# A list-scheduled sparse attention and feed-forward kernel: its planner gives each kind of DMA transfer its own share beside the weights, and the order is found anew

## The chip, the cores and the metric

The kernel runs on one core of a Trainium2 chip. The metric is the device time of one execution in microseconds. Five engines work from queues of their own: TensorE (PE, with its weight loads PEld), VectorE (DVE), ScalarE (ACT), GpSimd (POOL) and SyncE (SP). Each queue runs in the order in which it was written; engines wait for each other by semaphores. Transfers between HBM and SBUF are issued by SP, by ACT (four of them) and by GpSimd (the weights, which are cast to bf16 on the way).

## The reference

Attention over 4 batches of 8 heads, 768 positions and head dimension 64, where each query sees only its 6 best chunks of 32 keys; then a feed-forward layer on the 3072 tokens.

```python
ub = sum_d max(q * k_min[chunk], q * k_max[chunk])   # bound per query and chunk
ub = where(causal over chunks, ub, -1e9); top_chunks = the 6 largest
scores = q @ k.T / 8, masked to the chosen chunks and to the past
x = softmax(scores) @ v                               # tokens x 512
h = x @ w_in                                          # 512 -> 2048
out = (h * clip(h + 3, 0, 6) / 6) @ w_out             # 2048 -> 512
```

## The kernel before

The work is cut into 16 attention units (4 batches, two halves of the positions, two quads of heads; a unit is two pairs of heads) and 8 dense groups (batch and half: 384 tokens).

Attention of a unit: K and Q are loaded (`load_quad`, line 229, for batch 0; `load`, line 237, for the others in four parts each, KS and QS) and turned (line 375 on TensorE for batch 0; `KF` and `QF`, line 387, on VectorE for the others). VectorE takes minimum and maximum of each chunk of K (KMA, lines 400 to 403). TensorE forms the bounds (UBT, line 442), VectorE finds the 6 best chunks (lines 447 to 472), TensorE the scores (SPS, line 494 for batch 0, where the array is split by rows, line 497 for the others), ScalarE their exponentials (PT, line 507), GpSimd cuts the triangle of the diagonal (line 512), TensorE multiplies by V (PVP, line 530), and VectorE divides by the sums (Xb, line 542). V is loaded at lines 243 (VS, batch 0) and 248 (VT).

A dense group: its tokens are turned (XT, on TensorE at line 551, or for five groups through DRAM: BT, BD and BF, lines 561 to 580), then 16 times HP (four matmuls each, line 587), U (ScalarE, line 592) and GT (VectorE, line 595), then three times OP (16 matmuls each, line 602; the very last tile is cut in two, line 610), which is scaled and stored (lines 628 and 634). HP needs a half of WIN, OP needs a half of WOUT: the first 8 of its 16 matmuls the first half, the others the second.

Nothing of this order is written by hand. Every step is given to a `Plan` (`add`) with the engines that may run it and a length for each, a rank, the steps it waits for, and the buffers it takes and gives: four PSUM banks "m", two for scores, tiles in SBUF, and eight lanes for transfers under way. `order` then plays the steps as a list schedule: whenever an engine comes free in its own reckoning, the ready step with the lowest rank and with room goes next. The result is the order of each engine's queue; on the chip only the queue order and the semaphores are left. So every number in the plan (a rank, a length, a share) can change the order of all queues behind it. Ranks come from the unit or group, from the table RANK, and from the table SHIFT, which adds to the rank of single steps by their number.

The plan has a line of its own for transfers ("DMA") and one for weights ("WT"). While weights are under way or waiting, another transfer is reckoned at a fraction of its speed, 0.15, until the weights are through.

When a weight half is issued is ruled by a gate: GpSimd first copies one element of a tile that another transfer writes (`seen`, line 313), and only then issues the half (lines 316 and 319).

```python
GATE = dict(I0="V2", I1="I0", O0="I1", O1="O0")
```

I0 and I1 are the halves of WIN, O0 and O1 those of WOUT; V2 is the third unit's V. So before, each half is issued after the one ahead of it has landed.

Fillers: up to 45 us of the plan's time, where the plan sees TensorE idle for over 0.25 us, small matmuls on unused PSUM columns are put in (`occupy`, line 365).

Of the kernel before, what the change touches and what calls it, by code (L numbers as in the profile page):

```python
# [12 lines left out]
ACT = mybir.ActivationFunctionType  # L13
# [11 lines left out]


SHIFT = {
# [18 lines left out]
}  # L46


class Plan:
# [10 lines left out]
        self.room, self.steps = {kind: list(range(n)) for kind, n in room.items()}, []  # L60
        self.lane, self.lanes, self.lean = 0, room["lane"], {}

    def add(self, engine, length, rank, run=None, after=(), take=(), give=(), port=False, tiles=None, lock=None):


        step = dict(lengths=engine if isinstance(engine, dict) else {engine: length}, rank=(rank + SHIFT.get(len(self.steps), 0), len(self.steps)),
                    run=run, told=isinstance(engine, dict), port=port, tiles=tiles, lock=lock, take=take, give=give, then=[])
        step["wait"] = {e: len(after) for e in step["lengths"]}
        for other in after:
            other["then"].append(step)  # L70
        self.steps.append(step)
        return step
# [21 lines left out]
    def order(self, **busy):  # L94
# [19 lines left out]
        n = len(events)  # L114
        while events:
# [8 lines left out]
            for e, steps in ready.items():  # L124
                if free[e] > now + 1e-9:
                    continue
                for st in sorted(steps, key=lambda x: x["rank"][:1] if e == "DMA" else x["rank"]):
                    if "engine" in st:
                        steps.remove(st)
                    elif self.sooner(st, e, free, now):  # L130
                        continue
                    elif self.room_for(st):
                        steps.remove(st)
                        for held in st["take"]:
                            held[2] = self.take(held[0])
                        out.append(st)
                        begin = now
                        if e == "POOL" or e == "DVE" and st["port"]:
                            begin = max(now, port["DVE" if e == "POOL" else "POOL"])
                            port[e] = begin + st["lengths"][e]  # L140
                        begin = max(begin, locks.get(st["lock"], 0.0))
                        if e == "PE":
                            begin += 0.1 * (st["tiles"] != tiles)
                            tiles = st["tiles"]
                        length = st["lengths"][e]
                        if e == "PE" and begin < self.COLD:
                            length *= 1.9
                        if e == "DMA":
                            weights = max(free["WT"] - now, 0.0) + sum(x["lengths"]["WT"] for x in ready["WT"])
                            length = min(length / 0.15, weights + max(length - 0.15 * weights, 0.0))  # L150
                        st["at"], st["engine"], st["length"] = begin, e, length
                        free[e] = begin + st["length"]
                        if st["lock"]:
                            locks[st["lock"]] = free[e] + 0.12
                        n += 2
                        heapq.heappush(events, (free[e], n, st, True))
                        heapq.heappush(events, (free[e] + self.BEHIND[e], n + 1, st, False))
                        break
# [10 lines left out]
def kernel(  # L169
# [466 lines left out]


    SEQ = "K0 Q0 K1 Q1 Q3 Q2 K2 V1 V0 V2 K3 V3"
    GATE = dict(I0="V2", I1="I0", O0="I1", O1="O0")
    RANK = dict(lead2=-64.96, lead3=-10.65, rdense=58.76, step=10.99, fs=-0.34, rt=-2000.0, rw=-1999.0, lead=-10.68, sel=-8.96, opoff=45.01, opsp=1.83, tri=24.62, joint=-38.37, vals=-12.37, eb=-0.8, lp=-0.13, la=0.2, kc=5.02)  # L640
    plan = Plan(m=4, s=2, kf=3, qf=6, qr=6, ub=3, mt=3, pt=9, x=2, xt=2, bt=2, bd=2, gt=2, u=3, ot=2, vt=3, ks=2, qs=2, lane=8)
    plan.room["gt"].remove(1)
    add = plan.add
# [11 lines left out]
    def arrive(engine, issue, length, run, after=(), take=(), parts=1):  # L655
# [3 lines left out]
        for part in range(parts):  # L659
# [6 lines left out]
            if engine == "POOL":  # L666
                issued.append(got)
                got = add("GEN", 1.2, 0, after=[got])
            landed.append(add("WT" if engine == "POOL" else "DMA", length, 0, after=[got], give=lane))
        return landed  # L670

    held_inputs = {}
# [218 lines left out]
    for what in ("I0", "I1", "O0", "O1"):  # L891
        name, n = dict(I="WIN", O="WOUT")[what[0]], int(what[1])
        got, seen = landing[GATE[what]]
        there[name, n] = arrive("POOL", 0.95, 6.6 if name == "WIN" else 7.6, (load_weights, name, n, seen), after=got[-1:])
        landing[what] = there[name, n], lambda name=name, n=n: WIN[0:1, KT_HID - 1, n * DFF // 2:n * DFF // 2 + 1] if name == "WIN" else WOUT[0:1, n * FT // 2, 0:1]

    r = RANK["rdense"]
    for n_group, ((b, half), xs) in enumerate(finished.items()):
# [3 lines left out]
        if (b, half) in WORDS:  # L902
# [3 lines left out]
                                  take=[held_bt] if quad == 0 else [], give=[x]))  # L906
            lane = hold("lane")
            kept = add("SP", 0.37, -3000, later(keep_words, g), after=before, take=[held_bd, lane])
            kept, m = add("DMA", 1.4, 0, after=[kept], give=[held_bt, lane]), []
            for part in range(4):  # L910
                lane = hold("lane")
                m.append(add("SP", 0.43, -3000, later(fetch_words, g, part), after=[kept] + m[-1:], take=[held_bf, lane] if part == 0 else [lane]))
# [16 lines left out]
        for t in range(HB):  # L929
            prev = []  # L930
            m, ot = hold("m"), hold("ot")
            if b == B - 1 and half == 1 and t == HB - 1:
                m[1] = ot[1] = 2
                for part in range(2):
# [2 lines left out]
                    a = add(dict(ACT=0.36, DVE=0.35), None, r + RANK["rt"], later(result_last_out, g, t, part), after=prev, take=[] if part else [ot], give=[m])  # L937
                    lane = hold("lane")
                    a = add("SP", 0.37, -2000, later(result_last_store, g, t, part), after=[a], take=[lane])
                    add("DMA", 0.6, 0, after=[a], give=[ot, lane])  # L940
                continue
            for part in range(4):
                prev = [add("PE", 0.865, r + RANK["opoff"] + RANK["opsp"] * (4 * t + part), later(result, g, t, part),
# [2 lines left out]
            a = add(dict(ACT=0.56, DVE=0.66), None, r + RANK["rt"], later(result_scale, g, t), after=prev, take=[ot], give=[m])  # L946
            lane = hold("lane")
            a = add("SP", 0.37, -2000, later(result_out, g, t, nc.sync), after=[a], take=[lane])
            add("DMA", 0.75, 0, after=[a], give=[ot, lane])
        r += RANK["step"]  # L950
    for step in (steps := plan.order(PE=3.7, ACT=4.25, DVE=4.4, POOL=3.2, SP=3.7, DMA=1.6, WT=1.6)):
        chosen = {}
        for kind, _, number in step["take"]:
            chosen.setdefault(kind, []).append(number)
# [36 lines left out]
```

## Time and profile before

| | us |
|---|---|
| median of three runs | 272.17 (272.03 to 273.77) |
| the profiled execution | 271.37 |
| its span, first to last instruction | 269.7 |
| TensorE busy | 256.8 (95%) |
| VectorE busy | 209.4 (78%) |
| ScalarE busy | 191.6 (71%) |
| GpSimd busy | 128.7 (48%) |

The page gives busy time and share of the span of each engine, the span in 40 slices, the DMA queues, the chain of work that ended last, and the costliest groups of instructions with the idle time ahead of them. Matmuls are pipelined: a matmul's recorded time overlaps with the next one's, so what a matmul costs is better read from the time of a long run of them, divided by their count. TensorE's clock was granted in full in all 40 slices.

### The profile page before, as it was taken

The numbers are of one execution on the slowest core, as the hardware profiler recorded it, in microseconds if no ns is written. First come the engines' busy times: TensorE is split into PE (matmuls) and PEld (weight loads), VectorE is DVE, ScalarE is ACT, GpSimd is POOL, SyncE is SP. The second block draws the span as 40 slices with busy tenths as digits, with TensorE's granted clock in tenths as the row PEclk, the third lists the DMA queues.
The fourth block names the chain that finished last, engine by engine and source line by source line (L and its number), as shares of the span: only waits on it lengthen the run. The fifth ranks groups of instructions, "written<-read, shape, count | busy, mean of one in ns | idle before, by whom it ended". The sixth has DMA issues, their size and how long they took to land.

```text
span 269.7 us, 6517 instructions
## 1 busy us (share of the span) xinstructions
PE 256.8 (95%) x2350; PEld 152.7 (57%) x2373; DVE 209.4 (78%) x588; ACT 191.6 (71%) x306; POOL 128.7 (48%) x289
## 2 busy tenths in 40 slices
PE   7997999898999999999999999999999999999994
PEld 4645565654445677644664566654665756555443
DVE  7799898989799997899989999999894424857000
ACT  3589899685527899765984499953998874868021
POOL 4168579533767485559734666752842310200000
PEclk9999999999999999999999999999999999999999
DMA  8999999999948999954995599114103003201122
GB/s 166 219 198 188 190 175 154 176 149 185 212 108 117 127 157 176 186 164 139 150 159 141 157 155 181 40 60 139 39 4 117 5 38 139 58 0 41 39 78 79
DMA packets 122720, 33.71 MB, mean 125 GB/s; under 512 B 113216, under 2 KB 118080, under 8 KB 122688
## 3 DMA queue, kind: packets, MB, share of 16 engines
q1 hardware_dynamic: 117952, 28.71, 62.2%
q0 software_dynamic: 3136, 4.19, 9.5%
q10 hardware_dynamic: 1600, 0.39, 0.7%
q8 instruction: 18, 0.29, 0.6%
q14 instruction: 14, 0.11, 0.2%
HBM read 29.23 MB, written 8.26 MB: 139 GB/s over the span
## 4 chain that ended last, share of the span: by engine, by line
PE 73%; DMA 10%; DVE 8%; SPq 4%; ACT 2%; issue 1%; ACTq 0%; DVEq 0%
PE OP L602 28%; PE HP L587 23%; PE SPS L497 9%; DMA KS<-in_k_dram 8%; PE PVP L530 6%; PE UBT L442 4%; SPq L229 2%; DVE GT L595 2%; PE SPS L494 2%; DMA VS<-in_v_dram 2%; ACT PT L507 1%; PE OP L610 1%; SPq L237 1%; DVE KMA L401 1%; DVE KMA L400 1%
## 5 line engine op out<-in xcount | busy, mean ns | idle before, releaser
L587 PE MATMUL HP<-XT,WIN 128*128 128x384 bf16 x512 | 92.4, 326 | 2.4 <-DVE GT L595 2.3
L507 ACT ACTIVATE PT<-SPS 128x1024 bf16<-128x1024 f32 (+1 forms) x96 | 85.3, 927 | 12.0 <-PE SPS L497 9.9
L602 PE MATMUL OP<-WOUT,GT 128*128 128x512 bf16 x345 | 82.3, 379 | 1.9 <-issue 0.5
L592 ACT ACTIVATE U<-HP,THREE 128x384 bf16<-128x384 f32 x128 | 73.0, 594 | 15.1 <-PE HP L587 8.8
L595 DVE SCALAR_TENSOR_TENSOR GT<-U,HP 128x384 bf16<-128x384 bf16 x128 | 67.2, 545 | 14.9 <-ACT U L592 11.0
L587 PEld LDWEIGHTS <-WIN 128*128 128x128 bf16 x512 | 48.5, 98 | 34.4 <-issue 4.0
L602 PEld LDWEIGHTS <-GT 128*128 128x128 bf16 x368 | 35.1, 98 | 40.2 <-issue 3.7
L512 POOL TENSOR_SCALAR_AFFINE_SELECT PT<-PT 128x256 bf16<-128x256 bf16 x96 | 38.9, 418 | 35.9 <-ACT PT L507 34.9
L497 PE MATMUL SPS<-QLA,KL 128*128 128x384 bf16 (+2 forms) x240 | 36.3, 278 | 0.0
L628 ACT ACTIVATE OT<-OP 128x512 f32<-128x512 f32 x22 | 13.1, 597 | 27.4 <-PE OP L602 27.0
L331 POOL TENSOR_SCALAR_AFFINE_SELECT KL<-KF 64x384 bf16<-64x384 f32 x48 | 23.9, 501 | 14.4 <-DVE KF L387 12.1
L331 POOL TENSOR_SCALAR_AFFINE_SELECT QLA<-QF 64x384 bf16<-64x384 f32 x48 | 24.6, 512 | 12.2 <-DVE QF L387 6.3
L497 PEld LDWEIGHTS <-KL 128*128 128x128 bf16 x240 | 21.7, 98 | 12.8 <-issue 0.6
L530 PEld LDWEIGHTS <-PT 128*128 128x128 bf16 x672 | 23.9, 97 | 3.1 <-issue 0.4
L530 PE MATMUL PVP<-VB,PT 128*128 128x65 bf16 x672 | 25.6, 194 | 0.0
L411 ACT ACTIVATE QR<-QF 128x384 f32<-128x384 f32 x30 | 15.4, 531 | 9.4 <-DVE QF L387 9.3
L542 DVE TENSOR_TENSOR Xb<-PVP,RINV 128x384 bf16<-128x384 f32 x32 | 18.5, 579 | 1.1
L580 POOL COPY XT<-BF 128x384 bf16<-128x384 bf16 x20 | 9.3, 504 | 16.7 <-DMA BF<-BD 16.6
L536 DVE RECIPROCAL RINV<-PVP 128x6 f32<-128x6 f32 x32 | 5.9, 185 | 12.6 <-PE PVP L530 12.2
L387 DVE STREAM_TRANSPOSE KF<-KS 128x384 f32<-128x384 f32 x24 | 13.2, 560 | 1.7 <-DMA KS<-in_k_dram 1.3
L387 DVE STREAM_TRANSPOSE QF<-QS 128x384 f32<-128x384 f32 x24 | 12.8, 555 | 2.0 <-DMA QS<-in_q_dram 2.0
L400 DVE TENSOR_REDUCE KMA<-KF 128x12 f32<-128x384 f32 x24 | 13.1, 545 | 0.4
(80 smaller groups left out, 235.8 us busy)
## 6 DMA issues: line engine op xcount, KB each, us to landing
out_dram<-OT SPq DMA_DIRECT2D x23, 256.0 KB, 2.3
KS<-in_k_dram SPq DMA_DIRECT2D x24, 192.0 KB, 5.5
QS<-in_q_dram SPq DMA_DIRECT2D x24, 192.0 KB, 6.5
VT<-in_v_dram SPq DMA_DIRECT2D x24, 192.0 KB, 4.5
WIN<-in_moe_w_in_dram POOLq DMA_DIRECT2D x2, 1024.0 KB, 9.4
WOUT<-in_moe_w_out_dram POOLq DMA_DIRECT2D x2, 1024.0 KB, 10.1
BD<-BT SPq DMA_DIRECT2D x5, 384.0 KB, 2.4
BF<-BD SPq DMA_DIRECT2D x20, 96.0 KB, 2.3
```

Of the source, the lines that this page charges most:

```text
L331: nc.gpsimd.affine_select(out=to, in_=x, pattern=[[0, n]], compare_op=A.is_ge, fill=0.0, base=0, channel_multiplier=0)
L387: nc.vector.transpose(T[:], st[name][:, st["i"], half * HC:(half + 1) * HC, :].rearrange("p c e -> p (c e)"))
L400: nc.vector.tensor_reduce(out=over, in_=chunks, axis=X_AXIS, op=A.max)
L497: nc.tensor.matmul(SP[:, j, c0:c0 + n], lhsT=KLS[st["pair"] % 6][:, j, jb * P:(jb + 1) * P], rhs=st["QL", half][:, j, at:at + n], start=Tr ...
L507: nc.scalar.activation(PT[:, :, 0:cols], SP[:, :, 0:cols], ACT.Exp, scale=scale)
L512: nc.gpsimd.affine_select(out=PT[:, :, c0:c0 + P], in_=PT[:, :, c0:c0 + P], pattern=[[0, 2], [1, P]], compare_op=A.is_ge, fill=0.0, base=0 ...
L530: nc.tensor.matmul(PVP[:, j, n, :], lhsT=PT[:, j, c0:c0 + P], rhs=st["VB"][:, jb, j, :], start=(jb == 0), stop=(jb == qb))
L542: nc.vector.tensor_tensor(out=to, in0=PVP[:, :, :, 0:D], in1=RINV[:].to_broadcast([P, 2, HB, D]), op=A.mult)
L587: nc.tensor.matmul(HP[:], lhsT=WIN[:, kt, f * P:(f + 1) * P], rhs=g["XT"][:, kt, :, :], start=(kt == 0), stop=(kt == KT_HID - 1))
L592: nc.scalar.activation(U[:], g["HP", f][:], ACT.Relu, bias=THREE[:], scale=1.0)
L595: nc.vector.scalar_tensor_tensor(out=g["GT"][:, f, :], in0=g["U", f][:], scalar=6.0, in1=g["HP", f][:], op0=A.min, op1=A.mult)
L602: nc.tensor.matmul(g["OP", t][:], lhsT=g["GT"][:, f, t * P:(t + 1) * P], rhs=WOUT[:, f, :], start=(f == 0), stop=(f == FT - 1))
```

## The change

`add` takes a share for each step, and `order` uses it in place of 0.15. Input transfers with a length over 1 (the parts of K and Q of batches 1 to 3) get 0.09, the shorter ones 0.18, the store to DRAM of the turned groups 0.45, output stores 0.4, and all others 0.2. The lengths of the weights go from 6.6 and 7.6 to 6.3 and 7.3. The gates become V3, Q3, Q2 and O0: the first WIN half waits for the last V of batch 0, the second for the fourth unit's Q, the first WOUT half for the third unit's Q (both loaded before that V), and the second WOUT half for the first, as before. The SHIFT table is replaced whole (other steps, other numbers). The computation, its tiles and buffers stay. With these numbers the plan comes to another order on all five queues.

```diff
 SHIFT = {
-    4: -885.8, 6: -49.2, 8: -980.9, 10: -841.2, 12: -1020.7, 14: -50.4, 16: -1.5, 18: -911.2, 20: 8.9, 22: -4.1, 28: -823.6, 30: -2.5, 32: -915.5, 40:
...
+    16: -912.2, 40: 1266.8, 46: 1213.1, 89: 152.4, 91: 137.3, 99: 176.2, 100: -2962.9, 102: 115.3, 110: -1915.9, 120: 31.5, 123: -1888.8, 126: 110.3, 133:
...
 }
...
-    def add(self, engine, length, rank, run=None, after=(), take=(), give=(), port=False, tiles=None, lock=None):
+    def add(self, engine, length, rank, run=None, after=(), take=(), give=(), port=False, tiles=None, lock=None, share=0.2):
...
-                            length = min(length / 0.15, weights + max(length - 0.15 * weights, 0.0))
+                            length = min(length / st["share"], weights + max(length - st["share"] * weights, 0.0))
...
-    GATE = dict(I0="V2", I1="I0", O0="I1", O1="O0")
+    GATE = dict(I0="V3", I1="Q3", O0="Q2", O1="O0")
...
-            landed.append(add("WT" if engine == "POOL" else "DMA", length, 0, after=[got], give=lane))
+            landed.append(add("WT" if engine == "POOL" else "DMA", length, 0, after=[got], give=lane, share=0.09 if length > 1 else 0.18))
...
-        there[name, n] = arrive("POOL", 0.95, 6.6 if name == "WIN" else 7.6, (load_weights, name, n, seen), after=got[-1:])
+        there[name, n] = arrive("POOL", 0.95, 6.3 if name == "WIN" else 7.3, (load_weights, name, n, seen), after=got[-1:])
...
-            kept, m = add("DMA", 1.4, 0, after=[kept], give=[held_bt, lane]), []
+            kept, m = add("DMA", 1.4, 0, after=[kept], give=[held_bt, lane], share=0.45), []
...
-                    add("DMA", 0.6, 0, after=[a], give=[ot, lane])
+                    add("DMA", 0.6, 0, after=[a], give=[ot, lane], share=0.4)
...
-            add("DMA", 0.75, 0, after=[a], give=[ot, lane])
+            add("DMA", 0.75, 0, after=[a], give=[ot, lane], share=0.4)
```

More of the change, by code (lines that the diff above doesn't have):

```diff
@@ L61, in __init__ @@
         self.lane, self.lanes, self.lean = 0, room["lane"], {}
-    def add(self, engine, length, rank, run=None, after=(), take=(), give=(), port=False, tiles=None, lock=None):
+    def add(self, engine, length, rank, run=None, after=(), take=(), give=(), port=False, tiles=None, lock=None, share=0.2):
         step = dict(lengths=engine if isinstance(engine, dict) else {engine: length}, rank=(rank + SHIFT.get(len(self.steps), 0), len(self.steps)),
-                    run=run, told=isinstance(engine, dict), port=port, tiles=tiles, lock=lock, take=take, give=give, then=[])
+                    run=run, told=isinstance(engine, dict), port=port, tiles=tiles, lock=lock, share=share, take=take, give=give, then=[])
         step["wait"] = {e: len(after) for e in step["lengths"]}
@@ L948 @@
             a = add("SP", 0.37, -2000, later(result_out, g, t, nc.sync), after=[a], take=[lane])
-            add("DMA", 0.75, 0, after=[a], give=[ot, lane])
+            add("DMA", 0.75, 0, after=[a], give=[ot, lane], share=0.4)
         r += RANK["step"]
-    for step in (steps := plan.order(PE=3.7, ACT=4.25, DVE=4.4, POOL=3.2, SP=3.7, DMA=1.6, WT=1.6)):
+    steps = plan.order(PE=3.7, ACT=4.25, DVE=4.4, POOL=3.2, SP=3.7, DMA=1.6, WT=1.6)
+    for step in steps:
         chosen = {}
```

32 rows, old and new, of the table SHIFT are left out of this document.

## The prediction

> **What bounds the kernel now.** I read the page first, then windows cut at marks of the TensorE queue, then the chain, TensorE's waits and the queues by time.
>
> ```profile
> span 269.7 us, 6517 instructions
> ...
> DMA  8999999999948999954995599114103003201122
> ...
> 20.00:35.60 15.60, 13.55 (x215) 8.63 (x206) 13.92 (x53) 13.70 (x22) 10.97 (x23) 1.00 1.18 187
> 35.60:65.30 29.70, 27.18 (x270) 16.54 (x267) 26.91 (x58) 24.77 (x40) 17.70 (x39) 1.00 1.25 169
> 65.30:72.60 7.30, 7.23 (x43) 3.48 (x49) 6.66 (x14) 3.67 (x8) 3.46 (x9) 1.00 1.26 186
> 72.60:266.10 193.50, 191.83 (x1687) 113.37 (x1708) 145.97 (x409) 136.71 (x216) 88.67 (x193) 1.00 0.57 105
> ```
>
> A window's columns are its length, then busy time of PE, PEld, DVE, ACT and POOL. From 72.6 to 266.1 us TensorE idles 1.67 us of 193.5, at full clock (1.00). Both kernels hold the same matmuls but for fillers, so there an order can win little over a microsecond. What it can win lies before 72.6 us, where the DMA engines are nearly always busy and TensorE idles 2.05 us (20 to 35.6) and 2.52 us (35.6 to 65.3).
>
> ```profile
> 32.11 1.38 PE PVP L530 x42
> ...
> 33.92 0.78 PE XTP L551 x12
> 34.70 0.98 PE SPS L494 x16
> 35.68 1.41 PE HP L587 x8
> ...
> 65.31 0.38 PE OP L602
> ...
> 68.07 1.30 PE HP L587 x8
> 69.37 1.73 PE OP L602 x8
> ```
>
> These rows of the chain (start, length, what, count) give pitches: PVP 0.033 us, XTP 0.065, a row-split score 0.061, HP 0.163 (1.30/8), OP 0.216. HP starts at 35.6, OP at 65.3. Between them the queue of before holds 116 HP (18.9 us), 90 PVP (3.0), 48 row-split scores (2.9) and 12 XTP (0.8): 25.6 us of work in 29.7. So 4.1 us are lost, partly idle, partly in matmuls stretched where the row split switches. What stands behind it:
>
> ```profile
> PE HP L587 <- DVE GT L595: 2.3, 4, 1.2
> ...
> 58.24 0.58 DVE L387 STREAM_TRANSPOSE KF<-KS 128x384 f32<-128x384 f32 x1 [0.61 <-DMA KS<-in_k_dram]
> ...
> 69.66 0.58 DVE L387 STREAM_TRANSPOSE QF<-QS 128x384 f32<-128x384 f32 x1 [0.55 <-DMA QS<-in_q_dram]
> ```
>
> HP waits for a PSUM bank; the GT that frees it stands on VectorE's queue behind KF and QF, and these wait for loads that share the DMA engines with the weights.
>
> **The change part by part.** No instruction's work changes; the order does. I counted instructions in the new queues.
>
> *The first HP comes later.* Ahead of it stand 28 more row-split scores (1.7 us), 30 more PVP (1.0) and 7 more fillers:
>
> ```profile
> 7.27 1.06 PE L365 MATMUL QT<-IDENTB 128*128 128x128 bf16 x16
> ```
>
> Sixteen fillers take 1.06 us, so seven 0.5, together 3.2 us. ScalarE has four more exponentials (and two copies fewer) ahead of its first U and VectorE seven more instructions ahead of the first XT, so no engine is much sooner there: HP at 35.6 + 3.0 = 38.6. Only the fillers are loss; the rest is work done earlier.
>
> *The weights queue up.* The gate of the first WIN half moves from V2 to V3, those of the second half and of the first WOUT half to Q3 and Q2, which land long before. So GpSimd issues the second half right behind the first, and the first WOUT half after seven more triangles, near 31 us.
>
> ```profile
> 24.89 1.00 POOL L316 DMA_DIRECT2D WIN<-in_moe_w_in_dram  x1
> ...
> 26.27 0.56 POOL L257 TENSOR_SCALAR_AFFINE_SELECT VB<-VS 128x384 bf16<-128x384 f32 x1
> ...
> 34.53 0.77 POOL L316 DMA_DIRECT2D WIN<-in_moe_w_in_dram  x1
> DMA to landing us min/median/max: 9.1/9.4/9.6
> DMA to landing us min/median/max: 9.9/10.1/10.2
> q0 software_dynamic: 3136, 4.19, 9.5%
> ```
>
> The two landings are those of WIN and WOUT. A cast that needs V3 runs at 26.27, so V3 has landed by then; in the new SP queue the last V is the 34th load too. First WIN half: issue 26.4, landed 35.8, inside the 38.6 that HP waits for anyway. A queued half is not seen in this trace. Its packets take 6.4 us (9.5% of 269.7, a quarter of it); alone it needs 9.4 to 10.1. So it follows its predecessor by 6.4 to 10.0; I take 7.3 and 7.8, nearer to the packets, because issue (0.77 to 1.00) and landing then overlap. Second WIN half 43.1, first WOUT half 50.9; the second WOUT half, still gated by the first, 51 + 10.1 = 61.1 (58.7 to 65.4).
>
> The Trainium skill, "DMA: Bandwidth & Descriptors", section "Anatomy of one DMA — SWDGE (gpsimd) path", gives a DMA from GpSimd a fixed part of about 2.0 us, mostly the write receipt. By that a queued WIN half would follow after 7.4 us, and the sum would stay as it is.
>
> *The path to the first OP.* Between first HP and first OP the new queue has 96 HP (15.6), 60 PVP (2.0), 20 row-split scores (1.2) and 12 XTP (0.8): 19.6 us. Of the 4.1 us lost before I keep 1.0, since fewer scores are mixed in and no KF or QF stands between the last twelve GT. OP starts at 38.6 + 19.6 + 1.0 = 59.2. Its ninth matmul, at 60.9, needs the second WOUT half: landed 61.1, a wait of 0.2 (0 to 4.5). What is queued behind it is all of TensorE.
>
> *The loads of batch 1.*
>
> ```profile
> 27.98 13.23 SPq L237 DMA_DIRECT2D QS<-in_q_dram  x4
> 41.31 11.22 SPq L237 DMA_DIRECT2D KS<-in_k_dram  x4
> 52.57 13.23 SPq L237 DMA_DIRECT2D QS<-in_q_dram  x4
> ...
> 86.78 7.64 SPq L237 DMA_DIRECT2D QS<-in_q_dram  x4
> ```
>
> A K or Q part takes 1.9 us of the SP queue without weights (86.78) and 2.8 to 3.3 beside them; with the gaps between the weights taken out, about 4.0. Weights without gaps until 51 cost SP some 5 us of gap, 1.5 parts. But the second K now stands at places 7 to 10 of 16 instead of 9 to 12: issued by 51, on chip near 57, and VectorE asks for it only after the GT run, near 59. The last Q parts (13 to 16) arrive near 70, as before. Meanwhile TensorE has 32 OP (6.9) and 8 HP (5.2) that need no KF. I charge 0.8 us for GT behind a late QF; without that cover it would be up to 4.
>
> *Sum.* From first OP to first UBT of batch 1 the new queue has 40 OP (8.6) and 32 HP (5.2): 13.8 us, so UBT at 59.2 + 0.2 + 13.8 + 0.8 = 74.0. Before, it stood at 72.6 with 16 OP (3.5) fewer done, so the same work would be done at 76.1. The gain there is 2.1.
>
> *After it.* The first group that goes through DRAM has less cover:
>
> ```profile
> 72.61 1.45 PE UBT L442 x32
> ...
> 112.28 1.08 PE L530 MATMUL PVP<-VB,PT 128*128 128x65 bf16 x30
> ...
> 125.02 1.84 POOL L580 COPY XT<-BF 128x384 bf16<-128x384 bf16 x4
> ```
>
> From the group's last PVP to its XT went 13.5 us, and TensorE had work for it. The new queue has between the two 40 OP (8.6), one UBT (1.45) and twelve score matmuls (by OP's pitch a column 0.11 each, 1.3): 11.4. Up to 2.1 us can be missing; I take 0.6, since part of the 13.5 was VectorE's queue, which is shorter there. The later groups have 11 to 13 us, and at 11 the old kernel did not wait. The end is the same list of 32 half-width matmuls and two stores.
>
> So the gain is 2.1 - 0.6 = 1.5 us. The profiled execution took 271.37 us (span 269.7 and 1.7 around it), the median of the runs is 272.17, 0.8 above. The forecast is 272.17 - 1.5 = 270.7.
>
> **The rivals.**
>
> *The second half holds GpSimd (slower).* Nothing here shows a weight DMA issued while another still moves. If the issue must wait until the first has left the queue, GpSimd stands from 27.5 to about 35 with seven triangles behind it; the PVP that wants one of them goes from about 31 to 37 and TensorE, in order, with it. Price: 5.5 us after some slack, so 276.2. It decides as soon as the hold is over 3 us. Against it: each issue here took 0.77 to 1.00, but always on an empty queue.
>
> *WOUT is late (slower).* If a queued half follows by 9.5 to 10.0, that is, if nothing overlaps, the last half lands at 65.4 and the ninth OP waits 4.5 us, less the 0.8 it then hides: 274.4. For it speaks that the DMA engines are already full; against it the 6.4 us of packets.
>
> *Batch 1 starves.* If the parts of K and Q get less than the 4.0 us each says, KF waits past 59. With 5.5 us a part the second K lands near 62, GT is 3 us late and TensorE, with four banks, loses about 1.5: 272.2. The extreme is a strict turn of packets. One K or Q part has 1536 packets of 128 bytes; a weight half has 784 (3136/4). In turns, half a part would pass per weight half, six parts would be left when the last weight lands, and UBT would stand near 83: 280.
>
> For that extreme speaks the Trainium skill, "DMA: Bandwidth & Descriptors", section "Queues, rings and completion order": each DMA engine goes round robin between its queues, a packet at a time. By that rule, if its packets are the profile's, the row at 27.98 could not be, where four parts pass beside little more than one weight half. The trace does not agree.
>
> *More is won.* If none of the 1.0 + 0.2 + 0.8 + 0.6 I charged comes, 2.6 us more: 268.1; if half, 269.4. For it speaks that each of these waits has a cover of its own.
>
> *Nothing moves.* The order before 72.6 might only trade one wait for another, as the lost 4.1 us came from bank and VectorE order, not from one load: 272.2.
>
> **How the numbers follow.** Forecast (269.6 to 271.8): 0.45. More is won: 0.17. Nothing moves, or mild starving (271.8 to 273.5): 0.18. WOUT late: 0.10. GpSimd held: 0.08. Strict turns: 0.02. The range leaves out the two last and the far end of the wins: 268.4 to 274.9. One per cent, about what a measurement of this kernel can tell from no change, is 2.7 us: faster means under 269.4, slower over 274.9. Under 269.4: half of "more is won" and more, with a tail of the forecast, 0.16 + 0.08 = 0.24. Over 274.9: most of the held GpSimd, 0.4 of late WOUT, strict turns, 0.13, and 0.03 for a stall I don't see: 0.16. The rest, 0.60, lies within.
>
> **What would show it.** In the new profile: the two WIN issues about a microsecond apart near 26 to 28, each under 1.1 us; first HP at 38 to 39.5; landing of the second WIN half 15 to 17 us after its issue; first OP at 58 to 60.5, with little idle time between OP 8 and 9; first UBT of batch 1 at 73 to 75; idle TensorE before the HP of the first group through DRAM under 1 us; and under 2.5 us of idle time from there to the end. Wrong would make it: a WIN issue of several microseconds, OP waiting on WOUT for more than 2 us, VectorE's KF or QF waiting on loads for more than 3, or waits after 100 us that before did not have.

## The result, and the profile after

The changed kernel takes 283.5 us (median of four runs, 282.71 to 285.03) against 272.34 for the kernel before beside it: ratio 1.0404, 95% interval 1.0354 to 1.0453, so 11.2 us slower. The forecast of 270.7 us, a gain of 1.5, and its range (268.4 to 274.9) are missed on the slow side. The profiled execution took 283.24 us with a span of 281.5. In all that follows, medians are over all runs, and ratios leave out the runs that lie over 1.5% above the fastest of their kernel (one of e4, two of e3, one of e13).

The page, and windows cut at the same marks as before (length, then busy time of PE, PEld, DVE, ACT and POOL, the granted clock, the DMA share):

```profile
span 281.5 us, 6550 instructions
...
PEclk9998995799999999999999999999999999999999
DMA  8999999999333199997479689902313002401012
...
20.00:35.60 15.60, 13.03 (x182) 7.35 (x182) 11.75 (x54) 12.16 (x16) 9.85 (x23) 0.89 1.24 202
35.60:65.30 29.70, 22.13 (x249) 13.62 (x246) 18.95 (x44) 17.03 (x25) 11.78 (x25) 0.83 1.30 162
65.30:72.60 7.30, 7.30 (x45) 4.15 (x43) 6.28 (x12) 5.83 (x11) 0.00 (x0) 1.00 0.97 164
72.60:85.00 12.40, 12.40 (x71) 6.25 (x70) 11.74 (x26) 7.44 (x15) 9.60 (x21) 1.00 0.26 75
85.00:276.00 191.00, 189.09 (x1678) 110.24 (x1678) 142.30 (x406) 136.80 (x215) 89.74 (x195) 1.00 0.53 101
```

After 85 us TensorE idles 1.91 us of 191, as little as before. Between 35.6 and 65.3 it idles 7.57 us instead of 2.52, and its clock is 0.83 there instead of 1.00. The chain of waits names the place:

```profile
25.50 20.21 DMA KS<-in_k_dram
...
45.79 0.58 DVE KF L385
```

And the VectorE queue by time (start, length, line, what, count, idle time before it and its releaser):

```profile
36.59 0.56 DVE L540 TENSOR_TENSOR Xb<-PVP,RINV 128x384 bf16<-128x384 f32 x1
45.79 0.58 DVE L385 STREAM_TRANSPOSE KF<-KS 128x384 f32<-128x384 f32 x1 [8.65 <-DMA KS<-in_k_dram]
46.29 0.16 DVE L534 RECIPROCAL RINV<-PVP 128x6 f32<-128x6 f32 x1
46.48 0.56 DVE L540 TENSOR_TENSOR Xb<-PVP,RINV 128x384 bf16<-128x384 f32 x1
```

One K part is under way for 20.21 us. VectorE stands 8.65 us ahead of the KF that wants it. Before, the four parts of this K were issued at nearly the same time, and the same KF ran some ten microseconds sooner, with next to no wait:

```profile
22.27 5.61 SPq L237 DMA_DIRECT2D KS<-in_k_dram  x4
...
35.88 0.58 DVE L387 STREAM_TRANSPOSE KF<-KS 128x384 f32<-128x384 f32 x1 [0.46 <-issue]
```

Behind the late KF, in the same queue, stands an Xb of the first dense group. TensorE needs that Xb:

```profile
47.10 0.50 PE L549 MATMUL XTP<-IDENTB,Xb 128*128 128x128 bf16 x3 [7.47 <-DVE Xb L540]
...
49.35 4.73 PE L585 MATMUL HP<-XT,WIN 128*128 128x384 bf16 x16
...
71.04 1.24 PE L600 MATMUL OP<-WOUT,GT 128*128 128x512 bf16 x5
...
84.97 0.88 PE L440 MATMUL UBT<-QF,KMA 64*32 64x384 f32 x16
```

So the loss is made in one place, around the first HP (its wait, and the lowered clock in which the first 16 HP then take 4.73 us), and is handed on from there. What surrounds the late K, in the queues of GpSimd and of SP:

```profile
24.48 1.00 POOL L314 DMA_DIRECT2D WIN<-in_moe_w_in_dram  x1
25.60 0.75 POOL L314 DMA_DIRECT2D WIN<-in_moe_w_in_dram  x1
31.86 0.90 POOL L317 DMA_DIRECT2D WOUT<-in_moe_w_out_dram  x1
60.07 0.92 POOL L317 DMA_DIRECT2D WOUT<-in_moe_w_out_dram  x1
DMA to landing us min/median/max: 9.9/11.9/13.9
DMA to landing us min/median/max: 12.0/12.8/13.6
...
22.49 5.31 SPq L235 DMA_DIRECT2D KS<-in_k_dram  x4
27.89 17.19 SPq L235 DMA_DIRECT2D QS<-in_q_dram  x2
45.18 4.62 SPq L235 DMA_DIRECT2D KS<-in_k_dram  x4
```

The two landing rows are WIN and WOUT. The halves landed at 34.4 (24.48 + 9.9), 39.5 (25.60 + 13.9) and 45.5 us (31.86 + 13.6), and the K part at 45.7, close behind the third. In between SP got rid of two Q parts in 17.19 us; afterwards four K parts went in 4.62.

The packets of each queue say why. The DMA view of after, cut to 31 to 35 us, to 39.5 to 42 us, and to 46 to 58 us, when no weights move (q0 carries the weights, q1 all that SP issues; packets, MB, share):

```profile
q0 software_dynamic: 411, 0.81, 106.8%
q1 hardware_dynamic: 409, 0.05, 17.0%
...
q0 software_dynamic: 450, 0.46, 109.3%
q1 hardware_dynamic: 451, 0.06, 31.0%
...
q1 hardware_dynamic: 14263, 1.81, 148.8%
```

Beside queued halves the two queues pass the same number of packets, whatever their size: 2 KB of WIN (0.81 MB in 411) or 1 KB of WOUT against 128 bytes of K. Over the whole stretch from 29 to 43 us it is 1802 each. At 409 packets in 4 us a part of 1536 packets needs 15 us beside WIN, at 451 in 2.5 us it needs 8.5 beside WOUT, against 1.3 us without weights (14263 in 12).

### The profile page after: what moved, and what is told of

It reads as the page before. It is cut to its first block, busy times and chain, and to the rows that moved or that the text cites. A ratio compares the mean times of both kernels' runs of the same rounds, so it can differ in the third digit from the quotient of the medians.

```text
span 281.5 us, 6550 instructions
## 1 busy us (share of the span) xinstructions
PE 263.6 (94%) x2380; PEld 154.2 (55%) x2380; DVE 205.6 (73%) x586; ACT 192.8 (68%) x305; POOL 129.9 (46%) x292
## 4 chain that ended last, share of the span: by engine, by line
PE 46%; DMA 20%; DVE 17%; SPq 10%; ACT 2%; issue 2%; POOL 2%; ACTq 0%; DVEq 0%; POOLq 0%
PE HP L585 19%; PE OP L600 17%; DMA KS<-in_k_dram 11%; SPq L235 5%; DMA QS<-in_q_dram 4%; DVE GT L593 4%; PE SPS L495 3%; DVE KF L385 3%; SPq L227 2%; DVE KMA L398 2%; PE PVP L528 2%; DVE KMA L399 2%; DMA VT<-in_v_dram 2%; DMA BF<-BD 2%; PE UBT L440 2%
## 5 line engine op out<-in xcount | busy, mean ns | idle before, releaser
L505 ACT ACTIVATE PT<-SPS 128x1024 bf16<-128x1024 f32 (+2 forms) x96 | 85.0, 926 | 23.9 <-PE SPS L495 13.2
L600 PE MATMUL OP<-WOUT,GT 128*128 128x512 bf16 x368 | 84.7, 379 | 0.1
L585 PEld LDWEIGHTS <-WIN 128*128 128x128 bf16 x512 | 49.2, 99 | 33.7 <-issue 4.5
L510 POOL TENSOR_SCALAR_AFFINE_SELECT PT<-PT 128x256 bf16<-128x256 bf16 x96 | 38.6, 417 | 32.5 <-ACT PT L505 30.5
L495 PE MATMUL SPS<-QLA,KL 128*128 128x384 bf16 (+2 forms) x240 | 35.2, 278 | 0.7 <-ACT QLA L251 0.5
L528 PE MATMUL PVP<-VB,PT 128*128 128x65 bf16 x672 | 26.2, 194 | 0.0
L626 ACT ACTIVATE OT<-OP 128x512 f32<-128x512 f32 x20 | 11.9, 597 | 20.7 <-PE OP L600 20.5
L409 ACT ACTIVATE QR<-QF 128x384 f32<-128x384 f32 x29 | 14.8, 533 | 7.4 <-DVE QF L385 6.6
L255 POOL TENSOR_SCALAR_AFFINE_SELECT VB<-VT 128x768 bf16<-128x768 f32 x12 | 10.9, 908 | 8.9 <-DMA VT<-in_v_dram 7.9
L492 PE MATMUL SPS<-MT,EB 64*128 64x384 bf16 (+2 forms) x80 | 11.8, 310 | 2.9 <-ACT VB L251 1.3
```

The costliest lines, as they stand in the source:

```text
L409: nc.scalar.activation(QR[:], QF[:], ACT.Relu)
L495: nc.tensor.matmul(SP[:, j, c0:c0 + n], lhsT=KLS[st["pair"] % 6][:, j, jb * P:(jb + 1) * P], rhs=st["QL", half][:, j, at:at + n], start=Tr ...
L505: nc.scalar.activation(PT[:, :, 0:cols], SP[:, :, 0:cols], ACT.Exp, scale=scale)
L510: nc.gpsimd.affine_select(out=PT[:, :, c0:c0 + P], in_=PT[:, :, c0:c0 + P], pattern=[[0, 2], [1, P]], compare_op=A.is_ge, fill=0.0, base=0 ...
L528: nc.tensor.matmul(PVP[:, j, n, :], lhsT=PT[:, j, c0:c0 + P], rhs=st["VB"][:, jb, j, :], start=(jb == 0), stop=(jb == qb))
L585: nc.tensor.matmul(HP[:], lhsT=WIN[:, kt, f * P:(f + 1) * P], rhs=g["XT"][:, kt, :, :], start=(kt == 0), stop=(kt == KT_HID - 1))
```

## The experiments

Theory A: the halves queued behind each other starve K, and VectorE's order hands this to TensorE. A1 adds that the share goes by packets, A2 that it goes by bytes or time. Theory B: the new order costs the time by itself. Theory C: most of it is TensorE's lowered clock. In the diffs, `gates` names the tile whose landing each half's copy really reads, where it differs from the plan's; `move` puts steps, named by their numbers, ahead of another one in the finished order, and nothing else changes.

First marks of all profiled executions, read from the queues by time:

| | first KF | first HP | first OP | UBT | span |
|---|---|---|---|---|---|
| before | 35.88 | 35.61 | 65.31 | 72.53 | 269.7 |
| after | 45.79 | 49.35 | 71.04 | 84.97 | 281.5 |
| e5: before, halves queued | 45.55 | 35.10 | 75.36 | 82.58 | 281.4 |
| e1: after, halves spaced | 36.44 | 40.95 | 61.24 | 83.35 | 279.1 |
| e2: after, K's work later | 48.26 | 39.22 | 65.45 | 79.38 | 277.6 |
| e4: after, fillers | 43.98 | 47.36 | 67.91 | 81.84 | 277.7 |
| e7: after, 256-byte packets | 36.62 | 40.60 | 60.74 | 74.66 | 269.5 |
| e11: after, WIN in 512-byte packets | 37.38 | 43.03 | 63.20 | 77.12 | 274.9 |
| e3: after, second half behind K | 37.20 | 41.18 | 61.05 | 77.48 | 274.0 |
| e12: as e3, issued earlier | 36.70 | 44.70 | 64.66 | 78.59 | 276.3 |
| e13: as e12, placed better | 36.76 | 40.20 | 62.09 | 76.02 | 270.9 |
| e9: after, K before all weights | 40.87 | 46.20 | 66.33 | 80.25 | 276.8 |
| p1: after, old gates, planned anew | 36.18 | 40.49 | 58.31 | 73.55 | 281.0 |
| p2: before, new shares, planned anew | 36.10 | 35.51 | 57.25 | 73.69 | 296.4 |

**The queued halves, put into the old order (e5).**

```diff
 # kernel before; gates: I1="Q3", O0="Q2" in place of I1="I0", O0="I1"
+    move({987, 990}, 985)    # second WIN half, first WOUT half: right behind the first
```

> The kernel before, its order and numbers, but the second WIN half and the first WOUT half are issued right behind the first WIN half (their copies read the fourth and third unit's Q, landed long before); the last half waits for the first WOUT half as before. Theory A: the first K of batch 1, in time at 35.9 us before, lands at 43 to 47, its KF waits 7 to 11 us on VectorE with the GT of the first group behind it, TensorE fills its four banks and stands: first OP 6 to 10 us later than 65.3, total 278 to 283 us. Theory B (the new order is the cause, not the queued weights): KF waits under 1 us, 271 to 273.5 us. A mild form (loads slowed but still ahead of their use): KF waits 2 to 4 us, 273.5 to 277.

Measured: 283.06 us (282.51 to 283.74), ratio 1.0367 (1.0308 to 1.0426).

```profile
45.55 0.58 DVE L387 STREAM_TRANSPOSE KF<-KS 128x384 f32<-128x384 f32 x1 [10.64 <-issue]
...
49.69 1.44 PE L587 MATMUL HP<-XT,WIN 128*128 128x384 bf16 x4 [10.03 <-DVE GT L595]
```

With nothing but the queueing, the old order loses as much as the whole change does. KF comes 9.7 us later; its row names no transfer, but the longest K part of this run landed 20.1 us after its issue. TensorE has filled its banks and waits 10.03 us for the GT behind this KF. From 29 to 43 us the two queues passed 1831 and 1832 packets. That settles A against B for the early stage.

**The halves spaced again, in the new order (e1).**

```diff
 # kernel after; gates: I1="I0", O0="I1"
+    move({987}, 335)
+    move({990}, 562)
```

> The kernel after, its queues as they are, but the second WIN half is issued when the first has landed and the first WOUT half when the second WIN half has landed, each moved back on GpSimd's queue to a place that it reaches then (before KL's copy of EB, and before the third one). Theory A (the halves queued behind each other starve the loads of K, and VectorE's order hands this on): the first K of batch 1 lands at 34 to 37 us instead of 45.7, KF waits under 1 us instead of 8.65, HP starts at 39 to 40 instead of 49.35. OP then waits for the last WOUT half, which is landed near 66 as in the kernel before: 273 to 277 us, against 283.5 for after and 272.3 for before. Theory B (the new order of the queues costs the time by itself, whenever K lands): HP still after 47 us, 281 or more. Theory C (most of the loss is TensorE's lower clock, from which the wait is only the start): between, near 279, with a clock below 0.9 at 44 to 54 us though KF doesn't wait.

Measured: 282.01 us (280.77 to 283.45), ratio 1.0329 (1.0262 to 1.0396). K was in time (KF 36.44) and HP at 40.95, a microsecond later than A gave; the total is far over A's 273 to 277, for the new order wants the last half sooner than spaced halves bring it:

```profile
68.82 7.67 PE L600 MATMUL OP<-WOUT,GT 128*128 128x512 bf16 x24 [5.68 <-DMA WOUT<-in_moe_w_out_dram]
```

A wait there was expected, not its echo: the clock was 0.50 from 67 to 73 us, so that the 24 OP behind it took 7.67 us instead of 5.2 (0.216 each). The gain of one wait went into another.

**K's work moved behind (e2).**

```diff
 # kernel after
+    move({300, 306, 304, 305, 307, 311, 317, 315, 318, 316, 423, 432, 425, 426, 434, 435, 427, 428, 436, 437}, 1027)
```

> The kernel after with its gates, but the four KF of the first K of batch 1, their chunk limits and their KL casts moved as a block behind the GT of the first dense group's first half (VectorE and GpSimd; twenty steps, nothing else). Theory A: K lands at 45 to 46 us as in after, but no longer holds Xb: XTP at 38 to 39, HP at 39 to 40, TensorE's clock near 1.00 from 35 us on, OP near 60, UBT of batch 1 at 74 to 77, total 271 to 275 us. Theory B: HP at 39 but the time comes back at UBT because the late K and Q parts are what TensorE wants there in any case: UBT at 82 or later, 280 or more. Theory C (clock): the clock stays low from 26 us on, HP matmuls at 0.29 us instead of 0.163, total 277 to 280.

Measured: 279.14 us (278.96 to 279.93), ratio 1.0228 (1.0170 to 1.0285). HP started at 39.22, so it is the place of KF in VectorE's queue that carries the late K to TensorE. Only 4.4 us came back, less than A's 271 to 275, since the block of K's work now held GT:

```profile
54.68 0.89 PE L585 MATMUL HP<-XT,WIN 128*128 128x384 bf16 x4 [4.68 <-DVE GT L593]
```

**TensorE kept warm in the wait (e4).**

```diff
 # kernel after
+        if step["rank"][1] == 234:
+            occupy(104)
```

> The kernel after with 104 filler matmuls on TensorE between the last PVP ahead of the first XTP and that XTP, where TensorE stood idle for 7.5 us; the fillers take 6.9 us at full clock (1.06 us for 16). Nothing else changes, K lands at 45.7 us as before. Theory A alone (all of the loss is the wait): HP at 49.35, total 283 to 284 us, no change. Theory C (the idle stretch lowers TensorE's clock to 0.5 from 44 to 53 us and so costs about 3 us on top of the wait): clock 0.95 or more from 36 to 54 us, 16 HP in 2.6 to 3.5 us instead of 4.73, total 280 to 281.5 us.

Measured: 282.16 us (279.45 to 284.26), ratio 1.0358 (1.0280 to 1.0437). The profiled execution was the fastest, 279.45. Windows from 44 to 54 us, first after, then with fillers:

```profile
44.00:54.00 10.00, 6.90 (x35) 3.42 (x35) 7.08 (x16) 3.68 (x5) 5.58 (x12) 0.53 1.35 147
...
44.00:54.00 10.00, 8.68 (x98) 5.04 (x96) 9.86 (x23) 7.34 (x11) 7.27 (x17) 1.00 1.08 142
```

The clock held (1.00 against 0.53), and 16 HP took 2.90 us instead of 4.73. From KF to UBT it is 37.9 us instead of 39.2. So the clock is worth some 1.3 us in the profile and the wait the rest; C falls as the main cause. Of the 3.8 us between the two spans, 1.8 come from a K that landed earlier in this execution. The intervals of the two times overlap, so the timed runs alone don't show the 1.3.

**Packets of 256 bytes (e7).**

```diff
 # kernel after
-        nc.sync.dma_start(two[0][name][r:r + 32, :, :, :].rearrange("p i c d -> p (i c) d"),
-                          heads(x, two[0])[2 * j:2 * j + 2].rearrange("i (c p) d -> p (i c) d", p=CH)[:, :, 32 * e:32 * e + 32])
+        nc.sync.dma_start(two[0][name][r:r + 32, :, :, :].rearrange("p i c d -> p (i c d)").rearrange("p (c d) -> p c d", d=D),
+                          heads(x, two[0])[2 * j + e].rearrange("(c p) d -> p c d", p=CH))
```

The loads move the same bytes but leave out the arrangement that the scores need, so the kernel works on misplaced elements; the instructions behind them stay the same.

> The kernel after, but each K and Q part of batches 1 to 3 is fetched in 768 packets of 256 bytes instead of 1536 of 128 (the same 192 KB; the elements come in another order, so scores are of other data; all else is the same). Counted in the trace of after from 27 to 39 us, the weights' queue passed 1235 packets and SP's queue 1369: about one for one. Theory A1 (the DMA engines take turns by packets): the first K of batch 1 lands at 38 to 42 us instead of 45.7, its KF waits 1 to 5 us instead of 8.65, HP starts at 41 to 46 instead of 49.35, 274 to 280 us against 283.5. Theory A2 (the share goes by bytes or by time): a part needs as long beside the queued halves as before, K lands at 44 to 46, KF waits 7 us or more; what gets shorter is only what passes without weights, 280 to 283 us.

Measured: 270.9 us (269.95 to 271.97), ratio 0.9935 (0.9910 to 0.9959). From 27 to 39 us:

```profile
q0 software_dynamic: 973, 1.96, 88.0%
q1 hardware_dynamic: 1700, 0.43, 29.1%
```

After had 1369 packets and 0.17 MB on q1 there. The window also holds a stretch without weights; from 31 to 43 us, with both queues filled, they passed 1274 packets each, and q1 moved 0.32 MB instead of the 0.20 of after. So the share goes by packets, and A2 is out. K was there before VectorE asked, sooner than A1 gave, the time is below A1's 274 to 280, and the marks fall into place: HP 40.6, UBT 74.66. But this K hardly met the weights: its four parts, issued from 22.25 on, landed 4.2 to 5.8 us after their issue, and the weights' first packet moved at 28. It shows what a K in time is worth, not how it fares beside the halves; and wide packets also shorten every later K and Q part, so that not all of the 12.6 us need come from the first K.

**Weights in smaller packets (e11).**

```diff
-            nc.gpsimd.dma_start(WIN[:, :, c0:c1], moe_w_in[:, c0:c1].rearrange("(a p) n -> p a n", p=P))
+            for s0 in range(c0, c1, 256):
+                nc.gpsimd.dma_start(WIN[:, :, s0:s0 + 256], moe_w_in[:, s0:s0 + 256].rearrange("(a p) n -> p a n", p=P))
...
+    move({987}, 990)
```

> The kernel after with each WIN half fetched as four transfers of 256 columns (2048 packets instead of 512; same bytes, same place), the second half's four issues moved behind seven triangles on GpSimd's queue, so that triangles aren't held; WOUT as it was. Theory A1 (turns by packets): beside WIN, K's parts pass four times as many packets for each byte of weights: the first K lands at 34 to 38 us instead of 45.7, KF waits under 1.5 us, HP at 40 to 42. The halves land later (first near 36 to 38, second 44 to 47, first WOUT 50 to 53), and OP can wait for the last one by 0 to 4 us: 272 to 278 us. Theory A2 (share by bytes or time): K at 43 or later, KF waits 6 us or more, 280 to 284.

The last line moves the second half's issues behind seven triangles.

Measured: 276.1 us (275.05 to 277.22), ratio 1.0115 (1.0062 to 1.0168). The same lever from the other side, with K's packets as they were. From 28 to 34 us:

```profile
q0 software_dynamic: 1725, 0.85, 111.1%
q1 hardware_dynamic: 2754, 0.35, 52.9%
```

KF ran at 37.4 without a wait. From 31 to 33.5 us, with both queues filled, they passed 837 and 842 packets. But the move also left gaps: from 33.5 to 35 us it was 177 against 1822. So K gained by smaller packets and by gaps, and this run does not part the two. The issues on GpSimd's queue held a triangle, for which a PVP waited 1.90 us, so that HP came at 43.0 instead of 40 to 42; UBT was at 77.1, and the time is within what A1 gave.

**The second half behind K's landing (e3, e12, e13).**

```diff
 # e3; gates: I1="K4"
+    move({987, 990}, 304)
 # e12; gates: I1="K4", O1="Q2"
+    move({987, 990}, 335)
 # e13; gates as e12
+    move({232}, 335)
+    move({987, 990}, 335)
+    move({993}, 425)
```

> The kernel after, but the second WIN half waits for the first K of batch 1 to land (GpSimd's copy reads that K), and it and the first WOUT half, right behind it, stand at the KL casts of that K on GpSimd's queue. Beside the first K's four parts moves one weight half instead of three. Theory A1: K lands at 34.5 to 36.5, HP at 40 to 41 at clock 1.00. From 37 to 52 us two halves are queued and starve the second K and the Q parts; the last half is issued near 52 and lands at 62 to 64, OP waits 0 to 2 us; the Q parts come by 70 to 72: UBT of batch 1 at 75 to 79, 273 to 278 us. Theory B (the new order costs the time by itself): 281 or more with KF in time. If OP waits over 4 us as with the spaced halves, 280 to 282.

Measured: 274.64 us (272.96 to 279.88), ratio 1.0053 (1.0019 to 1.0086). K was in time and UBT at 77.5, as expected; HP at 41.2 and a wait of OP of 2.34 us for the last half are a little over the 41 and the 2 at most that were expected.

> The kernel after with the second WIN half behind the landing of the first K of batch 1, as in the run that gated it so (274.6 us, where OP waited 2.34 us for the last WOUT half), but this half and the first WOUT half stand two steps earlier on GpSimd's queue (before the second KL copy of EB), and the last half no longer waits for a landing. Theory A1: K in time, HP near 41; second half issued at 35.5 to 36.5 instead of 38.3, the last half at 48 to 52 and landed by 60 to 62; OP does not wait for it; UBT of batch 1 at 75 to 76.5 instead of 77.5: 271 to 273.5 us, about the kernel before. If the Q parts, behind three queued halves, come later than before and UBT waits for them: 274 to 277.

Measured: 278.14 us (276.75 to 278.86), ratio 1.0180 (1.0132 to 1.0228): a miss. I had put the two issues ahead of a triangle that TensorE needs at once:

```profile
40.34 0.85 PE L528 MATMUL PVP<-VB,PT 128*128 128x65 bf16 x22 [2.78 <-POOL PT L510]
```

> The kernel after with the second WIN half behind the landing of the first K, put with the first WOUT half behind the triangle that the earlier placing held up, ahead of the KL copy of EB; the last half waits for no landing and stands five KL casts earlier on GpSimd's queue. Theory A1: K in time, no PVP waits for a triangle, HP at 40.5 to 41.5; second half issued near 37, the last one at 42 to 48 and landed near 60, so that OP waits for none; the Q parts end near 68 as the queues hold the same transfers: UBT of batch 1 at 74.5 to 76.5, 270.5 to 273 us, the same as before within a per cent. If the Q parts come so late behind three halves that VectorE's QF waits over 2 us for them: UBT at 77 or later, 274 to 277 us.

Measured: 274.56 us (272.61 to 277.08), ratio 1.0062 (1.0029 to 1.0094). The marks were much as expected (HP 40.2, UBT 76.0), but they are those of the fastest of twelve runs, 272.61; the median is 1.5 us over the expected 273. It gives back most of the loss, as e3 does, so B, which asked for 281 or more with K in time, is out. It is still behind the kernel before, as is every version here that works on unchanged data.

**K before all weights (e9).**

```diff
 # kernel after; gates: I0="K4", I1="Q3", O0="Q2", O1="Q2"
+    move({984, 987}, 212)
```

> The kernel after, but no weight moves until the first K of batch 1 has landed: GpSimd's copy ahead of the first WIN half reads that K, and both WIN halves stand one place of three triangles later on GpSimd's queue; all four halves are then issued as GpSimd comes to them, with no further wait on a landing (the last one reads the third unit's Q too). Theory A1: K's four parts pass alone at 1.2 to 1.4 us each and land at 28 to 30; first WIN half issued near 30, landed at 39.5 to 41; HP at 40 to 41.5; the halves end at 46, 53 and 59, so that OP waits for none; ten K and Q parts are left then and end near 72. UBT of batch 1 at 75 to 78, 273 to 277 us. If GpSimd's wait for K holds the four triangles behind it and with them TensorE's PVP: HP 2 us later and 275 to 279. Theory B: 281 or more.

Measured: 277.88 us (277.38 to 278.55), ratio 1.0194 (1.0149 to 1.0239). K did come alone, but landed only at 31.7 instead of 28 to 30, HP came at 46.2, and the edit made a wait of its own: SP's Q loads overwrite the tile that the second half's copy reads, so SP stood until that copy at 33.4, with the DMA engines at a share of 0.56 from 28 to 36 us. It tells nothing of the new order.

**The parts of the change alone, through the planner (p1, p2).**

```diff
 # p1: kernel after
-    GATE = dict(I0="V3", I1="Q3", O0="Q2", O1="O0")
+    GATE = dict(I0="V2", I1="I0", O0="I1", O1="O0")
 # p2: kernel before, with the new shares and weight lengths
```

> The kernel after with the gates of before (each half waits for the one ahead of it), given to the planner, which makes its own order with the new shares, lengths and SHIFT numbers. Theory A: no half is queued behind another, so the first K lands by 36 and KF waits under 1 us; what is left is an order whose SHIFT numbers were found with other gates, 272 to 280 us. If the shares and SHIFT alone carry the loss (theory B): 282 or more.

Measured: 282.28 us (281.53 to 284.58), ratio 1.0368 (1.0306 to 1.0431).

> The kernel before with the new shares and the new weight lengths only, gates and SHIFT numbers as before; the planner makes its own order of them. Theory A: no half is queued behind another, KF waits under 2 us for the first K, whatever else the order brings: 271 to 279 us, the loss (if there is one) after 72 us. If the shares by themselves make the orders bad: over 280 with KF in time.

Measured: 297.97 us (297.21 to 299.88), ratio 1.0926 (1.0868 to 1.0985). Both are over what A gave: p1 lies where B was expected, p2 where the shares by themselves make a bad order. But in both K is in time (KF at 36.2 and 36.1) and the first UBT comes at 73.6 and 73.7; most of the loss comes later. From 130 to 200 us TensorE idles 10.6 us in p2 and 2.6 in p1, where the kernel before idles 0.6; what else p1 loses stays open. Each is an order of its own, for p1 runs the new SHIFT numbers with the old gates, p2 the old ones with the new shares. So they say little of the loss in after. That SHIFT numbers only fit the gates and shares that they were found for would explain both, and is not shown.

## Why the prediction was wrong, by its own steps

**The step that failed: the loads of batch 1.** It charged K and Q parts about 4.0 us each beside weights, 1.5 parts lost, and 0.8 us in all. Measured: some 15 us a part beside a WIN half, 8.5 beside a WOUT half, and 13.7 us at the first HP (49.35 instead of 35.61). It also looked at the wrong K. It followed the second K, asked for near 59, and did not see that the first K's last two parts now had three halves beside them instead of one, with their KF ahead of an Xb of the first dense group: of the four parts, issued from 22.49 on, the first two landed 4.4 and 5.4 us after their issue, the others 16.6 and 20.2. That is the wait that it left at nothing.

The 4.0 came from the issue times of the row at 27.98 (13.23 us for four parts). Such a row mixes two things: parts that creep beside a half, and parts that rush through in the gap between two halves. The old trace has both, apart, if the DMA view is cut: 33.5 to 36 us, in the gap, and 48 to 54 us, beside one half:

```profile
q1 hardware_dynamic: 3215, 0.41, 135.3%
...
q0 software_dynamic: 952, 0.97, 103.2%
q1 hardware_dynamic: 1011, 0.13, 26.1%
```

Two parts in 2.5 us there, two thirds of a part in 6 us here. To remove the gaps was to remove most of what the K parts lived on.

**The rival that came true** had 0.02: strict turns of packets, UBT near 83 and 280 us; measured 84.97 and 283.5. The Trainium skill, "DMA: Bandwidth & Descriptors", section "Queues, rings and completion order", gave its rule, and the prediction said that the trace did not agree. That judgement was wrong: 409 packets against 411 agree with turns by packets. The old trace agrees too, with a single half under way: from 28.5 to 32.5 us it has 393 packets of weights and 392 of K and Q, from 50 to 52 us 335 and 334. Windows that reach past the ends of a half show more on q1 (914 against 501 from 27 to 33 us, 1011 against 952 above). Fewer occur too: 12 against 193 from 38 to 40 us, with a Q part under way, for which nothing here gives the reason. The counts also don't tell whether a turn is one packet of the profile or several. That the total came so near is in part luck: the rival took 784 packets for every half and had UBT late by the parts left over at the end, while the loss came at the first HP.

**The plan shared the mistake.** Its own times, played through, put the fourth K part at 27.95 us with a length of 6.08, done at 34.03, and the KF just behind. The length is fixed when a transfer starts and counts the weights that are ready then. The second WIN half counts as ready from 28.05, a tenth of a microsecond later, and the WOUT half later still. With the second half alone the same formula gives 11.8 us. So a share of 0.09, low enough by itself (1.35 us of the plan become 15), acted on what was left of one half of three. That this is why the numbers settled on such an order is argued, not tried.

**The terms that held.** With K in time (e7) the path on TensorE comes out: first HP 40.6 (38.6 forecast), from there to OP 20.1 (20.6), from OP to UBT 13.9 (14.8). That the total fits as well, 270.9 (270.7), proves less, since e7 shortens every K and Q part; e3 and e13, with K in time and its packets as they were, took 274.6. The 2.0 us at HP go in part to the clock, 0.87 from 28 to 36 us. The first half was issued at 24.48, not at 26.4: its gate V3 is not the last V of batch 0 in the new queue, where V2 and V0 are loaded behind it. GpSimd was not held: the second issue took 0.75 us on a queue that was not empty, which ends that rival. A queued half followed its predecessor by 5.1 and 6.0 us (7.3 and 7.8 forecast), both under the range of 6.4 to 10.0. The last half was issued at 60.07 instead of 51, because GpSimd's queue stood behind the late K, and landed at 72.1; OP, as late itself, did not wait for it. After 85 us the waits of TensorE came to 1.91 us in all, so the 0.6 charged there was no mistake that counts. "Batch 1 starves" was priced by KF on the path to OP, where four banks hide some; the real path went by Xb, where nothing hides.

## What to carry to other kernels

Where two DMA queues are busy, cut the trace by queue and by time and count packets: in these traces a transfer in small packets beside one in large ones got as many packets, not as many bytes, and its own average hid that. Before transfers are queued closer, ask what lived in the gaps between them, and follow every consumer of it through the in-order queue that it stands in. A planner that fixes a transfer's length at its start does not see what is issued a moment later.

## What the runs showed of the hardware

TensorE's clock was not expected to matter. In after TensorE stands from 39.6 to 47.1 us:

```profile
42.00:43.00 1.00, 0.00 (x0) 0.00 (x0) 0.00 (x0) 0.00 (x0) 0.00 (x0) 1.00 1.44 218
43.00:44.00 1.00, 0.00 (x0) 0.00 (x0) 0.00 (x0) 0.00 (x0) 0.00 (x0) 0.56 1.38 208
...
52.00:53.00 1.00, 1.00 (x5) 0.49 (x4) 0.69 (x2) 0.58 (x1) 0.89 (x3) 0.50 1.62 144
53.00:54.00 1.00, 1.00 (x6) 0.35 (x3) 0.30 (x1) 0.58 (x1) 0.94 (x2) 0.82 1.52 143
```

The clock halves some 3.5 us into the idle stretch and comes back about 6 us after work resumes. So this stretch of 7.47 us, and the one of 5.68 us in e1, cost more than their length: 1.3 us here by e4, 2.5 in e1. The Trainium skill, "TensorE: Matmul & The Clock Gate", section "Part 1: The HAM clock gate", gives half clock after an idle window of about 3.4 us, and the trace agrees; for the way back it gives about 3.4 us of work, and here it took longer. Shorter waits can do it as well: in after the clock was 0.52 from 26 to 28 us, behind waits of 1.05 and 1.29 us with little work between them. In e13 it stayed at 1.00 there behind 1.57 and 1.28, so this dip comes in some executions and not in others.
